# Order of work where the gate and value layer begins: square-sum matmul one step later, a fifth split buffer, S4 and first pair sums deferred, narrowing at five steps

## The chip, the core and the metric

One core of one Trainium2 chip. The metric is the device time of one execution in microseconds; the median of three runs of the kernel before is 578.98 us. Engines are called TensorE (PE in the rows; PEld is its weight load), VectorE (DVE), ScalarE (ACT), GpSimd (POOL) and SyncE (SP), whose queue issues nearly all DMAs.

## What is computed

Causal attention (2 batches, 12 heads, 448 positions, head size 64), then two feed-forward layers over the 896 tokens. Weights arrive as float64 and the output is float32. The two layers, cut from the reference:

```
h = x @ w_in;  x = (h * np.clip(h + 3.0, 0.0, 6.0) / 6.0) @ w_out      # 768 -> 2048 -> 768
rms = np.sqrt(np.mean(x * x, axis=-1, keepdims=True) + 1e-06)
xn = x / rms * rms_g
g = xn @ w_gate;  val = xn @ w_val                                     # 768 -> 1536, twice
out = (g * (1.0 / (1.0 + np.exp(-g))) * val) @ w_out2                  # 1536 -> 768
```

## The kernel before

Features lie on the partitions and tokens on the free axis, in two halves g = 0 and 1 of 448 tokens. Every float32 product is made of three matmuls of 128x128 by 128x448 (`mm3`): weight high part by data high part (L204 of the program before), high by low (L206), low by high (L208). So each weight and each operand has to be split beforehand: a ScalarE cast gives the high part (`whi`, `yhi`), a VectorE subtraction the low part (`wlo`, `ylo`).

A weight piece of 128x768 goes through: a load of 768 KB (`raw`, three buffers, shared with the pieces `braw` of w_out2 and `praw` of the later gate and value weights), the narrowing from float64 by two ScalarE passes (L155, L159) and a VectorE join (L164), then the split (L180, L186). `w_low` issues the load three pieces ahead. Pieces used a second time, for token half 1, come back as float32 (`c`) from a copy in memory (`kept`). `whi` and `wlo` have NW = 4 buffers each.

The order is written out by hand. All engines' work is emitted in steps; a step holds nine matmuls behind the attention, and `at(d, f)` puts f into the step d steps on. What a step emits for an engine stands ahead of that step's matmuls, and each engine works off its own list in order. The stages on TensorE are attention beside the first layer for half 0 (`ff1_in`), `ff1_in` for half 1, `ff1_out` for halves 0 and 1 (tiles y0_0 to y0_5 and y1_0 to y1_5, 16 x 3 matmuls each, weights 32 to 47 and 48 to 63), the gate/value layer's plain part `ff2_plain` (tiles f, 18 matmuls each, weights 64 to 69), its part by Strassen's scheme (`ff2_strassen`, three matmuls times three for each product), and the last layer (`strassen`).

`ff2_plain` goes through f0_0 to f0_3, f1_0 to f1_3, then f0_4, f1_4, f0_5, f1_5 (first number the token half, second the weight less 64; even is gate, odd value). A gate tile goes through Silu on ScalarE (`ff2_gate`), a value tile is multiplied to it on VectorE (`ff2_val`).

The norm of a token half: ScalarE scales and squares each y tile (`ff1_y`), the squares are added up, one matmul n with a matrix of ones sums over the partitions (`rms_sum`, L596), a square root on ScalarE and a reciprocal on VectorE follow (`rms_root`, L600, L601), then products with y (`y_scale`, L613) and splits (`y_split`, `y_low`, L626). For half 0 this lies far ahead of its use; for half 1 n is issued inside f0_0 and the first tile that reads its result is f1_0. Operands of the Strassen part are differences and sums of y tiles (`y_sums`, `y_more`): sets 5, 7, 6 and 3, the last (S4) read last. `sums_first` and `sums_second` make such sums of the finished gate-value products, in pairs p, and store them for the last layer (`left`).

`b_prepare` loads a piece of w_out2, `b_narrow` narrows it, `b_join` and `b_sums` derive seven matrices from it and store them (`kept`). Twelve pieces are taken, six beside `ff1_in` of half 1 and six beside `ff1_out` of half 1 (every 3.7 steps).

Of the kernel before, what the change touches and what calls it, by code (L numbers as in the profile page):

```python
# [21 lines left out]
NK = DM // 128  # L22
# [10 lines left out]
PLAIN = 3  # L33
MASK = -8e9
NRAW, NC_BUF, NW = 3, 3, 4
# [14 lines left out]
def fused_kernel(ctx: ExitStack, tc, qa, qb, ka, kb, v, w_in, w_out, w_gate, w_val, w_out2, rms_g, out):  # L50
# [38 lines left out]

    def begin_step():  # L90
        now = clock["now"]
        while due[now]:
            fn, args = due[now].pop(0)
            fn(*args)
        del due[now]
# [18 lines left out]
    apart = {n: APART for n in range(NW - 1)}  # L114
# [97 lines left out]
    def b_prepare(column, part):  # L212

        raw = wpool.tile([128, 768, 2], U32, tag="raw", name=f"braw{column}_{part}", bufs=NRAW)
        nc.sync.dma_start(raw.rearrange("p n t -> p (n t)"), w_out2[2 * column + part].bitcast(U32))
        at(3, b_narrow, column, part, raw)
# [224 lines left out]
    def ff1_out(g, w0):  # L441


        for m in range(NK):
            ps = psum(f"y{g}_{m}")[:, :NT]
            for k in range(NF1):
                i = m * NF1 + k
                yield from mm3(ps, w_tile(w0 + i // 6, i % 6), gs[g, k], k == 0, k == NF1 - 1)
            at(1, ff1_y, g, m, ps)
        for k in range(NF1):  # L450
            gs.pop((g, k))
# [11 lines left out]
    def left_ready(g, m, t):  # L463
# [6 lines left out]
        if all((i, 2 * p + j) in left for i in range(2) for j in range(2)):  # L470
            at(1, sums_first, p)
# [105 lines left out]
    def ff1_y(g, m, ps):  # L577
# [5 lines left out]
        if m == 0:  # L583
            ri[g] = s
        elif m < NK - 1:
            at(1, rms_add, g, s)
        else:
            nc.vector.tensor_add(ri[g], ri[g], s)
            at(1, rms_sum, g)
# [9 lines left out]
    def rms_root(g, ps):  # L599
        nc.scalar.activation(ri[g], ps, AF.Sqrt, bias=eps, scale=1.0 / DM)  # L600
        nc.vector.reciprocal(ri[g], ri[g])  # L601
        for i, k in enumerate((0, 1, 2, 3, 4, 5)):
            at(1 + (i // 2 if g else 2 * i), y_scale, g, k)
# [35 lines left out]
    def y_more(j):  # L639
        a11, a12 = ys.pop((0, j)), ys.pop((0, j + KH))  # L640
        nc.vector.tensor_sub(a11, ys.pop((1, j + KH)), a11)
        nc.vector.tensor_sub(a12, a12, a11)
        at(1, y_split, 6, j, a11)
        at(2, y_split, 3, j, a12)
# [4 lines left out]
    def ff2_plain(w0):  # L649
# [3 lines left out]
        for t, (g, i) in enumerate(order):  # L653
# [3 lines left out]
            if t == 0:  # L657
                at(1, w_split)
            elif t in (5, 6) or t >= 8 and t % 2 == 0:
                splits.pop(w0 + (t - 5 if t < 8 else i - 1), None)  # L660
                at(1, w_split)
            elif t == 7:
                splits.pop(w0 + 2)
# [115 lines left out]
    def ff2_strassen():  # L779
# [7 lines left out]
        for q, m in order:  # L787
            if q == 1 and m + 1 < NF2:
                pair_begin(m + 1)
            if q == 1 and m + 1 == NF2:  # L790
# [3 lines left out]
                for n in range(NW - 1):  # L794
                    at(4 + n, w_split)
# [74 lines left out]
    def products():  # L870
# [3 lines left out]
        yield from ff1_out(0, 2 * NP1)  # L874
        plan_preps(PREPS[0][2], *PREPS[1])
# [5 lines left out]
    with tc.manual_schedule():  # L881
# [40 lines left out]
        for n in range(NW - 1):  # L922
# [74 lines left out]
```

## Time and profile before

| | us |
|---|---|
| median of three runs | 578.98 (578.37 to 579.11) |
| the profiled execution's own time | 582.0 |
| its span, first to last instruction | 580.2 |
| TensorE busy | 566.5 (98%) |
| VectorE busy | 409.5 (71%) |
| ScalarE busy | 376.0 (65%) |
| GpSimd busy | 105.1 (18%) |
| mean granted TensorE clock | 0.994 of full |
| DMA | 125.59 MB, mean 216 GB/s |

The rows come from the one profiled execution, so sums of rows stand against 582.0 and not against the median. Times in a row count from the start of the span. A matmul's duration in a row includes its pipeline; the distance from one start to the next is what TensorE spends on it.

### The profile page before, as it was taken

The numbers are of one execution on the slowest core, as the hardware profiler recorded it, in microseconds if no ns is written. First come the engines' busy times: TensorE is split into PE (matmuls) and PEld (weight loads), VectorE is DVE, ScalarE is ACT, GpSimd is POOL, SyncE is SP. The second block draws the span as 40 slices with busy tenths as digits, with TensorE's granted clock in tenths as the row PEclk, the third lists the DMA queues.
The fourth block names the chain that finished last, engine by engine and source line by source line (L and its number), as shares of the span: only waits on it lengthen the run. The fifth ranks groups of instructions, "written<-read, shape, count | busy, mean of one in ns | idle before, by whom it ended". The sixth has DMA issues, their size and how long they took to land.

```text
span 580.2 us, 9124 instructions
## 1 busy us (share of the span) xinstructions
PE 566.5 (98%) x3057; PEld 493.6 (85%) x3057; DVE 409.5 (71%) x783; ACT 376.0 (65%) x740; POOL 105.1 (18%) x148
## 2 busy tenths in 40 slices
PE   8899999999999999999999989899999999999997
PEld 6457777777899999999999779799999999999996
DVE  4766777776467786555585679988797887865871
ACT  7997888887576588776564776546555555554540
POOL 4665535353000000010010100120112110000000
PEclk9999999999999999999999999899999999999999
DMA  8958776753369889985687842373654647576751
GB/s 235 280 186 248 223 250 199 250 177 111 132 218 298 292 295 323 326 317 203 215 297 246 323 156 87 113 253 121 201 175 162 206 153 260 171 237 205 266 183 63
DMA packets 51231, 125.59 MB, mean 216 GB/s; under 512 B 6768, under 2 KB 30256, under 8 KB 51184
## 3 DMA queue, kind: packets, MB, share of 16 engines
q1 hardware_dynamic: 50752, 124.66, 64.3%
q8 instruction: 24, 0.39, 0.3%
q10 hardware_dynamic: 432, 0.34, 0.2%
q14 instruction: 23, 0.19, 0.1%
HBM read 93.36 MB, written 31.62 MB: 215 GB/s over the span
## 4 chain that ended last, share of the span: by engine, by line
PE 82%; DVE 6%; DMA 4%; ACT 4%; SPq 3%; issue 2%; DVEq 0%
PE h L208 7%; PE h L204 7%; PE h L206 7%; PE y L208 6%; PE y L204 6%; PE y L206 6%; PE f L208 4%; PE f L204 4%; PE f L206 4%; PE o L391 3%; PE t L365 3%; PE s L314 3%; PE fr L208 2%; PE fx L204 2%; PE fx L208 2%; PE fr L206 2%
## 5 line engine op out<-in xcount | busy, mean ns | idle before, releaser
L186 DVE TENSOR_TENSOR wlo<-c,whi 128x768 fp32r<-128x768 f32 x91 | 90.4, 996 | 24.2 <-ACT whi L180 21.7
L180 ACT CAST whi<-c 128x768 fp32r<-128x768 f32 x91 | 76.1, 837 | 46.9 <-DVE c L164 25.9
L208 PE MATMUL h<-xh,wlo 128*128 128x448 f32 x192 | 72.0, 375 | 0.0
L204 PE MATMUL y<-ghi,whi 128*128 128x448 f32 x192 | 70.5, 367 | 0.6 <-ACT whi L180 0.6
L208 PE MATMUL y<-ghi,wlo 128*128 128x448 f32 x192 | 70.5, 367 | 0.5 <-DVE wlo L186 0.5
L206 PE MATMUL h<-xl,whi 128*128 128x448 f32 x192 | 70.9, 369 | 0.0
L204 PE MATMUL h<-xh,whi 128*128 128x448 f32 x192 | 70.4, 367 | 0.0
L206 PE MATMUL y<-glo,whi 128*128 128x448 f32 x192 | 69.4, 361 | 0.0
L349 POOL TENSOR_SCALAR sm<-sm,st 112x112 f32<-112x112 f32 (+1 forms) x96 | 55.9, 600 | 68.3 <-ACT pt L375 28.8
L331 ACT ACTIVATE sm<-sm,st 112x112 f32<-112x112 f32 (+3 forms) x96 | 49.9, 532 | 3.5 <-DVE st L324 3.4
L164 DVE SCALAR_TENSOR_TENSOR c<-c,raw 128x768 uint32<-128x768 uint32 x38 | 38.5, 1014 | 18.6 <-ACT raw L159 12.4
L208 PEld LDWEIGHTS h<-xh,wlo 128*128 128x128 f32 x192 | 36.0, 188 | 9.3 <-issue 6.7
L592 POOL TENSOR_TENSOR sq<-sq,sq 128x448 f32<-128x448 f32 x8 | 10.3, 1286 | 175.4 <-DVE c L164 94.7
L157 POOL TENSOR_SCALAR praw<-praw 128x768 uint32<-128x768 uint8 x18 | 19.3, 1074 | 122.7 <-DMA praw<-in_w_gate 74.9
L324 DVE CUSTOM_DVE_ANT_0 sm<-s,mask 112x112 f32<-112x112 f32 (+3 forms) x96 | 37.3, 443 | 5.9 <-PE s L314 5.7
L208 PEld LDWEIGHTS y<-ghi,wlo 128*128 128x128 f32 x192 | 35.9, 187 | 5.0 <-DVE wlo L186 1.6
L204 PEld LDWEIGHTS y<-ghi,whi 128*128 128x128 f32 x192 | 36.0, 188 | 3.5 <-ACT whi L180 1.0
L206 PEld LDWEIGHTS h<-xl,whi 128*128 128x128 f32 x192 | 36.0, 188 | 2.8
L206 PEld LDWEIGHTS y<-glo,whi 128*128 128x128 f32 x192 | 36.0, 188 | 2.8
L204 PEld LDWEIGHTS h<-xh,whi 128*128 128x128 f32 x192 | 36.2, 188 | 2.5
L428 DVE SCALAR_TENSOR_TENSOR t<-t,h 128x448 f32<-128x448 f32 x32 | 19.8, 618 | 24.5 <-ACT t L424 24.5
L365 PE MATMUL t<-ident,sm 112*112 112x112 f32 x240 | 33.1, 269 | 2.9 <-POOL sm L349 2.4
(169 smaller groups left out, 1353.7 us busy)
## 6 DMA issues: line engine op xcount, KB each, us to landing
raw<-in_w_in SPq DMA_DIRECT2D x16, 768.0 KB, 5.3
raw<-in_w_out SPq DMA_DIRECT2D x16, 768.0 KB, 6.3
braw<-in_w_out SPq DMA_DIRECT2D x12, 768.0 KB, 7.0
c<-kept SPq DMA_DIRECT2D x21, 384.0 KB, 3.3
a<-left SPq DMA_DIRECT2D x35, 224.0 KB, 3.9
praw<-in_w_gate SPq DMA_DIRECT2D x9, 768.0 KB, 4.4
praw<-in_w_val SPq DMA_DIRECT2D x9, 768.0 KB, 5.7
keptin<-c SPq DMA_DIRECT2D x16, 384.0 KB, 2.7
```

The lines of the kernel that those rows point to most:

```text
L157: nc.gpsimd.tensor_scalar(low, byte, 1.0 / 32.0, -15.5 / 32.0, op0=ALU.mult, op1=ALU.add)
L164: nc.vector.scalar_tensor_tensor(bits, bits, 3, z, ALU.logical_shift_left, ALU.bitwise_or)
L180: nc.scalar.copy(hi, c)
L186: nc.vector.tensor_sub(lo, c, f32(hi))
L204: nc.tensor.matmul(ps, whi, xhi, start=first, stop=False, skip_group_check=again)
L206: nc.tensor.matmul(ps, whi, xlo, start=False, stop=False, skip_group_check=again)
L208: nc.tensor.matmul(ps, wlo, xhi, start=False, stop=last, skip_group_check=again)
L324: nc.vector.tensor_tensor_reduce(dst, src, mask[:, S - n:], scale=-0.125, scalar=3e38, op0=ALU.add, op1=ALU.min, accum_out=st[u][:, 0, c:c ...
L331: nc.scalar.activation(dst, dst, AF.Exp, scale=-1.0, bias=st[u][:, 0, c:c + 1], accum_out=st[u][:, 1, c:c + 1])
L349: nc.gpsimd.tensor_scalar(t[:, o:o + n], t[:, o:o + n], c, 1.0, op0=ALU.mult, op1=ALU.mult)
L365: nc.tensor.transpose(banks[-1][:C, o:o + C], t[:, o0 + kc * C:o0 + (kc + 1) * C], ident[:C, :C])
L428: nc.vector.scalar_tensor_tensor(t, t, 1.0, ps, ALU.min, ALU.mult)
```

## The change

It edits the order at several places, and one count of buffers:

- NW goes from 4 to 5, with one more `w_split` emitted as `ff1_out` of half 1 begins; every later split then runs one piece further ahead. `ff2_plain` and `ff2_strassen` have their calls of `w_split` rearranged for that. Where NW - 1 = 3 stood for the first splits, NRAW = 3 stands now, the same number.
- `b_narrow` comes five steps after the load instead of three, for all twelve pieces.
- `ff1_y` is put at the head of the next step (`soon`) instead of behind what is there.
- `rms_sum` comes a step later.
- S4 (the last subtraction of `y_more`, now `y_last`) and its split come 12 and more steps later.
- The sums of the first pair (`sums_first(0)`) come 12 steps later instead of one.

What it does to the lists of the engines, at three places. The first is ScalarE's list beside `ff1_out` of half 1 (y1), before and after. The names braw4_1 and braw5_1 are the last two pieces of w_out2, whi59 to whi63 the casts of weights for y1.

```order
L180 CAST whi59_3660<-c59_3565 128x768
L180 CAST whi60_3696<-c60_3598 128x768
L155 ACTIVATE braw5_1_3672<-braw5_1_3672 128x768
L159 ACTIVATE braw5_1_3672<-braw5_1_3672 128x768
L180 CAST whi61_3723<-c61_3634 128x768
L579 ACTIVATE y1_3_3726<-y1_3_3618,gvec_74 128x448
L581 ACTIVATE sq1_3_3728<-y1_3_3618 128x448
L180 CAST whi62_3761<-c62_3683 128x768
L180 CAST whi63_3793<-c63_3709 128x768
```

```order
L184 CAST whi60_3650<-c60_3560 128x768
L159 ACTIVATE braw4_1_3590<-braw4_1_3590 128x768
L163 ACTIVATE braw4_1_3590<-braw4_1_3590 128x768
L184 CAST whi61_3692<-c61_3599 128x768
L583 ACTIVATE y1_3_3725<-y1_3_3617,gvec_74 128x448
L585 ACTIVATE sq1_3_3727<-y1_3_3617 128x448
L184 CAST whi62_3731<-c62_3634 128x768
L159 ACTIVATE braw5_1_3662<-braw5_1_3662 128x768
L163 ACTIVATE braw5_1_3662<-braw5_1_3662 128x768
L184 CAST whi63_3758<-c63_3671 128x768
```

The casts whi61 and whi62, and y1_3's passes, stood behind the narrowing of braw5_1 and now stand ahead of it; the same holds for the earlier pieces.

The second is where half 1's norm begins. TensorE's list, with n1 the square-sum matmul and f0_0, f0_1 the first gate and value tile, before and after:

```order
L206 MATMUL f0_0_3884<-ylo2_2_3595,whi64_3836 128x448
L596 MATMUL n1_3916<-sq1_0_3424,ones_70 128x448
L208 MATMUL f0_0_3884<-yhi2_2_3594,wlo64_3837 128x448
L204 MATMUL f0_1_3920<-yhi1_0_3399,whi65_3864 128x448
L206 MATMUL f0_1_3920<-ylo1_0_3400,whi65_3864 128x448
```

```order
L210 MATMUL f0_1_3922<-ylo1_2_3491,whi65_3846 128x448
L600 MATMUL n1_3931<-sq1_0_3414,ones_70 128x448
L212 MATMUL f0_1_3922<-yhi1_2_3490,wlo65_3847 128x448
L208 MATMUL f0_1_3922<-yhi2_0_3532,whi65_3846 128x448
L210 MATMUL f0_1_3922<-ylo2_0_3533,whi65_3846 128x448
```

n1 moved by nine matmuls, from f0_0 into f0_1. ScalarE's list behind it, from the square root before, and from the Silu of f0_0 (t0_0) after:

```order
L600 ACTIVATE sq1_0_3424<-n1_3916,eps_73 128x448
L180 CAST whi67_3931<-c67_3901 128x768
L685 ACT_TABLE_LOAD
L685 ACTIVATE t0_0_3934<-f0_0_3884 128x448
L619 CAST yhi0_0_3960<-y1_0_3422 128x448
L619 CAST yhi0_1_3963<-y1_1_3523 128x448
L619 CAST yhi0_2_3980<-y1_2_3636 128x448
L619 CAST yhi4_0_3983<-y1_3_3726 128x448
L619 CAST yhi4_1_3998<-y1_4_3812 128x448
```

```order
L695 ACTIVATE t0_0_3933<-f0_0_3894 128x448
L604 ACT_TABLE_LOAD
L604 ACTIVATE sq1_0_3414<-n1_3931,eps_73 128x448
L623 CAST yhi0_0_3972<-y1_0_3412 128x448
L623 CAST yhi0_1_3975<-y1_1_3506 128x448
L623 CAST yhi0_2_3990<-y1_2_3626 128x448
L623 CAST yhi4_0_3993<-y1_3_3725 128x448
L695 ACT_TABLE_LOAD
L695 ACTIVATE t0_1_3998<-f0_2_3947 128x448
L159 ACTIVATE c68_4000<-raw68_3862 128x768
L163 ACTIVATE raw68_3862<-raw68_3862 128x768
L623 CAST yhi4_1_4012<-y1_4_3805 128x448
```

The Silu of f0_0 moved ahead of the square root, which adds two table loads, and the narrowing of weight 68 (c68, raw68) moved ahead of the last two casts (yhi4_1, yhi4_2) that f1_0 reads.

The third is VectorE's list around wlo68, the low part of the weight that f0_4 reads, before and after; ylo5, ylo6, ylo7 and ylo3 are operands of the Strassen part, ylo4 of f1_0.

```order
L690 TENSOR_TENSOR t1_0_4078<-f1_1_4054,t1_0_4078 128x448
L626 TENSOR_TENSOR ylo3_1_4121<-y0_4_3253,yhi3_1_4120 128x448
L626 TENSOR_TENSOR ylo6_2_4127<-y0_2_3091,yhi6_2_4126 128x448
L186 TENSOR_TENSOR wlo68_4131<-c68_4080,whi68_4130 128x768
L164 SCALAR_TENSOR_TENSOR c69_4133<-c69_4133,raw69_3914 128x768
L626 TENSOR_TENSOR ylo3_2_4148<-y0_5_3334,yhi3_2_4147 128x448
L186 TENSOR_TENSOR wlo69_4169<-c69_4133,whi69_4168 128x768
```

```order
L630 TENSOR_TENSOR ylo4_0_3994<-y1_3_3725,yhi4_0_3993 128x448
L168 SCALAR_TENSOR_TENSOR c68_4000<-c68_4000,raw68_3862 128x768
L630 TENSOR_TENSOR ylo4_1_4013<-y1_4_3805,yhi4_1_4012 128x448
L630 TENSOR_TENSOR ylo4_2_4016<-y1_5_3903,yhi4_2_4015 128x448
L637 TENSOR_TENSOR y1_3_3725<-y1_0_3412,y1_3_3725 128x448
L638 TENSOR_TENSOR y1_0_3412<-y0_0_2912,y1_0_3412 128x448
L700 TENSOR_TENSOR t0_1_3998<-f0_3_3979,t0_1_3998 128x448
L190 TENSOR_TENSOR wlo68_4034<-c68_4000,whi68_4033 128x768
```

wlo68 moved from behind the split passes of the Strassen operands to the place right behind the product t0_1 of f0_3; the passes ylo3 went far behind it.

The diff:

```diff
--- before.py
+++ after.py
@@ -31,8 +31,9 @@
 NSLOT = 79
 PREPS = (2, 4, 6), (1, 3.7, 6)
 PLAIN = 3
+LATE = 12
 MASK = -8e9
-NRAW, NC_BUF, NW = 3, 3, 4
+NRAW, NC_BUF, NW = 3, 3, 5
 
 BESIDE, AFTER = 4.8, 9
 APART = 4
@@ -86,6 +87,9 @@
 
     def at(delay, fn, *args):
         due[clock["now"] + delay].append((fn, args))
+
+    def soon(fn, *args):
+        due[clock["now"] + 1].insert(0, (fn, args))
 
     def begin_step():
         now = clock["now"]
@@ -111,7 +115,7 @@
     srcs += [(p, n) for p in ORDER for n in range(NN)]
     raws, plain, splits = {}, {}, {}
 
-    apart = {n: APART for n in range(NW - 1)}
+    apart = {n: APART for n in range(NRAW)}
     state = {"load": 0, "split": 0, "limit": OUT2}
 
     def w_load():
@@ -213,7 +217,7 @@
 
         raw = wpool.tile([128, 768, 2], U32, tag="raw", name=f"braw{column}_{part}", bufs=NRAW)
         nc.sync.dma_start(raw.rearrange("p n t -> p (n t)"), w_out2[2 * column + part].bitcast(U32))
-        at(3, b_narrow, column, part, raw)
+        at(5, b_narrow, column, part, raw)
 
     def b_narrow(column, part, raw):
         c = f32(raw[:, :, 1])
@@ -446,7 +450,7 @@
             for k in range(NF1):
                 i = m * NF1 + k
                 yield from mm3(ps, w_tile(w0 + i // 6, i % 6), gs[g, k], k == 0, k == NF1 - 1)
-            at(1, ff1_y, g, m, ps)
+            soon(ff1_y, g, m, ps)
         for k in range(NF1):
             gs.pop((g, k))
 
@@ -468,7 +472,7 @@
         if q:
             left_keep(q, p, t)
         if all((i, 2 * p + j) in left for i in range(2) for j in range(2)):
-            at(1, sums_first, p)
+            at(1 if p else LATE, sums_first, p)
 
     def sums_first(p):
 
@@ -586,7 +590,7 @@
             at(1, rms_add, g, s)
         else:
             nc.vector.tensor_add(ri[g], ri[g], s)
-            at(1, rms_sum, g)
+            at(2, rms_sum, g)
 
     def rms_add(g, s):
         nc.gpsimd.tensor_add(ri[g], ri[g], s)
@@ -599,8 +603,8 @@
     def rms_root(g, ps):
         nc.scalar.activation(ri[g], ps, AF.Sqrt, bias=eps, scale=1.0 / DM)
         nc.vector.reciprocal(ri[g], ri[g])
-        for i, k in enumerate((0, 1, 2, 3, 4, 5)):
-            at(1 + (i // 2 if g else 2 * i), y_scale, g, k)
+        for k in range(NK):
+            at(1 + (k // 2 if g else 2 * k), y_scale, g, k)
         if g:
             for j in range(KH):
                 at(6 + j, y_sums, j)
@@ -637,11 +641,15 @@
         at(1, y_more, j)
 
     def y_more(j):
-        a11, a12 = ys.pop((0, j)), ys.pop((0, j + KH))
+        a11 = ys.pop((0, j))
         nc.vector.tensor_sub(a11, ys.pop((1, j + KH)), a11)
-        nc.vector.tensor_sub(a12, a12, a11)
         at(1, y_split, 6, j, a11)
-        at(2, y_split, 3, j, a12)
+        at(LATE + j, y_last, j, a11)
+
+    def y_last(j, s2):
+        a12 = ys.pop((0, j + KH))
+        nc.vector.tensor_sub(a12, a12, s2)
+        at(1, y_split, 3, j, a12)
 
 
     ss, spare = {}, []
@@ -654,13 +662,15 @@
             m, n = divmod(i, 2)
             if t < 2:
                 splits.pop(w0 + t - 2, None)
-            if t == 0:
+            if t == 3:
                 at(1, w_split)
-            elif t in (5, 6) or t >= 8 and t % 2 == 0:
-                splits.pop(w0 + (t - 5 if t < 8 else i - 1), None)
+            elif t == 5:
+                splits.pop(w0)
                 at(1, w_split)
-            elif t == 7:
-                splits.pop(w0 + 2)
+            elif t in (6, 7):
+                splits.pop(w0 + t - 5)
+            elif t in (8, 10):
+                splits.pop(w0 + i - 1)
             if t == len(order) - 6:
                 at(1, pair_load, PLAIN, 0)
                 at(2, pair_load, PLAIN, 1)
@@ -792,7 +802,7 @@
                 for n in range(NRAW):
                     at(1 + n, w_load)
                 for n in range(NW - 1):
-                    at(4 + n, w_split)
+                    at(4 + n + 3 * (n // 3), w_split)
                 for p in range(NF2 // 2):
                     at(1 + p // 2, a_fetch, ORDER[0], p)
                     at(4 + p // 2, a_split, ORDER[0], p)
@@ -872,6 +882,7 @@
         plan_preps(0, *PREPS[0])
         yield from ff1_in(1, NP1)
         yield from ff1_out(0, 2 * NP1)
+        at(1, w_split)
         plan_preps(PREPS[0][2], *PREPS[1])
         yield from ff1_out(1, 3 * NP1)
         yield from ff2_plain(IN2)
@@ -919,7 +930,7 @@
         for n in range(NRAW):
             plan[12 + 12 * n].append((1, w_load))
             plan[52 + 6 * n].append((1, w_load))
-        for n in range(NW - 1):
+        for n in range(NRAW):
             plan[26 + 12 * n].append((0, w_split))
 
         work = products()
```

## Rows read from the trace of the kernel before

**Rows 1.** The page, part 1: busy us, share of the span, instructions.

```profile
PE 566.5 (98%) x3057; PEld 493.6 (85%) x3057; DVE 409.5 (71%) x783; ACT 376.0 (65%) x740; POOL 105.1 (18%) x148
```

**Rows 2.** TensorE's waits: who waited for whom, us, times, longest.

```profile
PE f L208 <- DVE wlo L186: 2.0, 1, 2.0
PE n L596 <- DVE sq L588: 1.9, 1, 1.9
```

**Rows 3.** Timeline of TensorE, 337 to 353: start, us, operation, [idle before <-releaser].

```profile
338.07 0.36 PE L206 MATMUL f<-ylo,whi 128*128 128x448 f32 x1
340.29 1.02 PE L596 MATMUL n<-sq,ones 128*128 128x448 f32 x2 [1.86 <-DVE sq L588]
...
341.35 0.36 PE L204 MATMUL f<-yhi,whi 128*128 128x448 f32 x1
...
352.27 0.36 PE L204 MATMUL f<-yhi,whi 128*128 128x448 f32 x1
```

**Rows 4.** Timeline of TensorE, 310 to 325.

```profile
311.06 0.36 PE L206 MATMUL y<-glo,whi 128*128 128x448 f32 x1
...
311.74 0.36 PE L204 MATMUL y<-ghi,whi 128*128 128x448 f32 x1
...
321.84 0.37 PE L208 MATMUL y<-ghi,wlo 128*128 128x448 f32 x1
322.81 0.47 PE L204 MATMUL y<-ghi,whi 128*128 128x448 f32 x1 [0.60 <-ACT whi L180]
...
324.02 0.47 PE L208 MATMUL y<-ghi,wlo 128*128 128x448 f32 x1 [0.54 <-DVE wlo L186]
324.33 0.37 PE L204 MATMUL y<-ghi,whi 128*128 128x448 f32 x1
```

**Rows 5.** Timeline of TensorE, 366 to 378.

```profile
367.03 0.37 PE L206 MATMUL f<-ylo,whi 128*128 128x448 f32 x1
369.40 0.65 PE L208 MATMUL f<-yhi,wlo 128*128 128x448 f32 x1 [2.00 <-DVE wlo L186]
...
373.09 0.36 PE L204 MATMUL f<-yhi,whi 128*128 128x448 f32 x1
```

**Rows 6.** Stretch 370:371: busy (x) by engine, PEclk, DMA share, GB/s.

```profile
370.00:371.00 1.00, 1.00 (x5) 0.87 (x4) 0.75 (x2) 0.70 (x1) 1.00 (x1) 0.50 0.00 0
```

**Rows 7.** Timeline of ScalarE, 304 to 330.

```profile
320.35 0.91 ACT L155 ACTIVATE braw<-braw 128x768 f32<-128x768 f32 x1 [8.06 <-DMA braw<-in_w_out]
321.16 0.88 ACT L159 ACTIVATE braw<-braw 128x768 uint32<-128x768 uint8 x1
```

**Rows 8.** DMA issues: xcount, KB each, median us to landing.

```profile
braw<-in_w_out SPq DMA_DIRECT2D x12, 768.0 KB, 7.0
...
raw<-in_w_gate SPq DMA_DIRECT2D x3, 768.0 KB, 6.4
```

**Rows 9.** Timeline of VectorE, 335 to 395.

```profile
342.02 2.95 DVE L601 RECIPROCAL sq<-sq 128x448 f32<-128x448 f32 x1
...
346.08 0.95 DVE L186 TENSOR_TENSOR wlo<-c,whi 128x768 fp32r<-128x768 f32 x1
...
349.62 3.30 DVE L626 TENSOR_TENSOR ylo<-y,yhi 128x448 fp32r<-128x448 f32 x6
...
368.39 0.95 DVE L186 TENSOR_TENSOR wlo<-c,whi 128x768 fp32r<-128x768 f32 x1
```

**Rows 10.** Timeline of ScalarE, 335 to 395.

```profile
341.35 0.64 ACT L600 ACTIVATE sq<-n,eps 128x448 f32<-128x448 f32 x1 [0.24 <-PE n L596]
...
342.99 1.28 ACT L685 ACT_TABLE_LOAD   x1
344.28 0.55 ACT L685 ACTIVATE t<-f 128x448 f32<-128x448 f32 x1
...
347.60 2.18 ACT L619 CAST yhi<-y 128x448 fp32r<-128x448 f32 x4 [0.83 <-DVE y L613]
```

**Rows 11.** Timeline of SP's DMA queue, 310 to 340.

```profile
334.11 0.33 SPq L124 DMA_DIRECT2D raw<-in_w_gate  x1
```

## The prediction, made blind

> **What bounds the kernel now.** I read the page first: TensorE is busy for 98% of the span [rows 1], so the only time that can be won is time in which it stands or is granted less clock. Second, its list of waits: the two longest single ones are a wait of 2.0 us for wlo and one of 1.9 us for the square-sum, each happening once [rows 2]. Third, the timeline of TensorE around these places, which gives the loss in steps between matmuls. A matmul normally starts 0.202 us after the one before: from 341.35 to 352.27 there are 54 of them [rows 3]. Four places lose time, all between 311 and 373 us.
>
> - y half 1, output tile 4, wlo58: 311.06 to 311.74 is two steps, 0.68 instead of 0.40 us: 0.28 lost [rows 4].
> - The same tile, whi61 and then wlo61: 321.84 to 324.33 is four steps, 2.49 instead of 0.81: 1.68 lost [rows 4].
> - The square-sum matmul n of half 1: after the matmul at 338.07 it should start at 338.27 and starts at 340.29: 2.02 lost [rows 3].
> - The gate tile f of half 0, fifth column, wlo68: 367.03 to 373.09 is eleven steps, 6.06 instead of 2.22: 3.84 lost [rows 5]. Only some 2.2 us of this is the wait. After TensorE had stood there, the granted clock was 0.50, the 1.2 GHz level of the two (2.4 is the other) [rows 6]; the steps stay slow until 373.09. A wait that goes takes this tail with it.
>
> Together 7.82 us. What ended each wait is on other engines. At 320.35 ScalarE had stood 8.06 us for the load of a w_out2 piece [rows 7]: the narrowing is placed three steps after the load's issue, a step is nine matmuls, so 5.5 us, and such a load takes 7.0 us at the median [rows 8]. The cast of whi61 stood behind it. The square-sum waited because ScalarE squares the last y tile only at the end of a chain of narrowings that the same late start pushed back. wlo68 was last in a VectorE queue that runs without a gap from the reciprocal at 342.02 to 368.39 [rows 9].
>
> **The change part by part.**
>
> *Narrowing at five steps, and one split more in flight.* Five steps are 9.1 us, over the 7.0 us of the load [rows 8]. In the order, whi59 to whi62 each move ahead of a narrowing that they followed, and the fifth buffer and the additional split at the start of the y half 1 move each split two steps (3.6 us) forward. So whi61 no longer waits for the load of the last piece, and I book 0.28 + 1.68 = 1.96 us. What this adds is that a raw buffer is held two steps longer, and SP's loads of the next raw pieces stand behind that release. The pieces come 3.7 steps apart through three buffers, so one is due again after 11 steps and is released after 6. The stores of the derived pieces move later on SP's queue by the same two steps; nothing reads them until the last layer. I cost both at 0, with the two steps (3.6 us) as cover. In the first half, where the same delay is applied, TensorE has no wait now and none is booked; the bounds are 0 and what is lost at a like place, 1.68 us.
>
> *Square-sum a step later.* n moves nine matmuls back, 1.82 us, and y and its square are now put at the head of their step. ScalarE's two passes for y (not moved on TensorE) come before the last cast of w. The margin becomes 1.82 us from the move and some 3.6 us from the earlier chain, against a wait of 2.02. It goes: 2.02 us. n and everything that hangs on it stay; the question is what is late next, since the products of half 1 now start earlier after n: 352.27 less 340.29 is 11.98 us now [rows 3], and 11.98 - 1.82 = 10.16 us after the change.
>
> Count from n's start. The square root starts at +1.06 [rows 3, 10]. The order puts a Silu and a table load in front of it, which are new there. The Silu needs the gate tile that ends 1.62 us before n (eight matmuls); Silu 0.55 and load 1.28 [rows 10] end at about +0.4. So it is hidden by 0.6 us. The reciprocal takes +1.73 to +4.68 (342.02, 2.95 long) [rows 9]. The first ylo started at 349.62, +9.33 [rows 9]; the pass of wlo67 that lay before it (0.95 long, 0.87 of the queue) [rows 9] is now done earlier, so +8.46, finished by +9.1. TensorE reads it with its second matmul, +10.36. The last two ylo are the tight ones, since the order puts the second new table load, a Silu, both narrowing passes of the next weight and their join in front of them. On ScalarE the fourth yhi ends at about +7.5 (four products 0.54 apart after +4.7, then its own 0.57); load 1.28, to +8.8; Silu 0.55, to +9.35; two passes of 0.91 and 0.88 [rows 7], overlapping by a tenth, to +11.0; VectorE's join, 0.95 as for a tile of this size [rows 9], to +12.0; the fifth ylo to +12.6. Its reader is the 14th matmul of the tile, 10.16 + 13 x 0.202 = +12.8. So it is hidden by 0.2 us, and the sixth by about as much. I take 0. The other end is a lateness of about 1 us if ScalarE is half a microsecond later at two places.
>
> The Trainium skill, "ScalarE: Activation LUTs", section "What ACT_TABLE_LOAD costs", gives 1.28 us for the load and a further 1.38 us of drain for each switch of table set. The trace agrees on the load alone: it ends at 344.27 and the Silu starts at 344.28, with nothing between [rows 10]. By the Trainium skill's figure the change would end near the time of the second rival.
>
> *S4, pair sums and their stores later.* Three subtractions and two split passes leave VectorE's queue ahead of wlo68, and the split of weight 68 is issued two tiles (7.3 us) earlier: wlo68 now stands right behind the product of the fourth tile. In the count above that is near +15, and its reader comes four tiles after the first of half 1, at 10.16 + 14.6 = +24.8. So 3.84 us go, tail included. The deferred passes, ten of about 0.6 us on VectorE (the four sums among them) and three casts on ScalarE, land in the stretch from 375 to 395, where the order has them before their readers by 6 us or more; I cost them at 0. The four stores leave SP's queue ahead of the loads of the next pairs, which can only come sooner.
>
> *The sum.* 1.96 + 2.02 + 3.84 = 7.82 us gained, nothing booked against it. The profiled execution took 582.0 us, so 574.2 on its scale. The median of the runs is 578.98, 3.0 us less than that, so some of the waits may be shorter without the profiler. I choose the whole sum, because the two largest terms hang on the order of queues and not on a load: 578.98 - 7.82 = 571.2.
>
> **The rivals.**
>
> *The waits on loads are smaller in a plain run.* The missing 3.0 us would lie in the terms that hang on loads (1.96 and 2.02). Then only 7.82 - 3.0 = 4.8 us are to be had: 574.2. For it speaks the 8.06 us stand of ScalarE, which rests on a single slow load [rows 7]. Against it: the 3.0 us can lie anywhere in the first 50 us too.
>
> *A new wait before the first tile of half 1.* The cover is 0.2 us. Suppose each switch of table held ScalarE for twice its row, 1.28 us more. The first load would end at -0.5 instead of -1.8, the Silu at 0.0, the second load at +2.6, so the square root 1.5 us late, and the last casts another 1.3: 2.8 us. TensorE would wait 2.6 us there and then run at the lower clock as after 369.40, another 1.67 (3.84 less 2.17): 571.2 + 4.3 = 575.5. Against it: the Silu that follows the load at once [rows 10]. The drain in the Trainium skill's page "ScalarE: Activation LUTs" would be such a hold.
>
> *The wait moves.* If the next weight (69) or the pair after it inherited the lateness of wlo68 and the square root that of n, the kernel would stay at about 579.0. Against it: the queue ahead of these got shorter too.
>
> *Slower, by the load of weight 68.* Its narrowing now stands on ScalarE ahead of two casts that the first tile of half 1 reads, where it stood far behind them. If that load landed late, TensorE would stand behind it one for one. It is issued at 334.11 [rows 11], takes 6.4 us at the median [rows 8], so lands by 340.5, and is needed at about 347.5. It decides from there on: to end slower than 578.98 by 1.2 us, the wait must be 7.82 + 1.2 - 1.67 = 7.35 us, so a landing at about 355. No load in the trace is near that.
>
> **How the numbers follow.** Forecast 0.70 (571.2, itself 570.0 to 572.5); smaller waits 0.15 (574.2); new wait 0.06 (575.5); the wait moves 0.05 (579.0); slower 0.04 (580.2 or more). The first two hold 0.85, so the range goes from 569.9 to 575.2. A measurement of this kernel tells 0.2%, 1.2 us, from no change: faster 0.70 + 0.15 + 0.06 = 0.91, the same 0.05, slower 0.04.
>
> **What would show it.** Right: in the list of waits of TensorE none for wlo, whi or the square-sum is left, the granted clock stays at 1.00 through 360 to 380, ScalarE's rows have two more table loads of 1.28 us, and the first tile of half 1 starts some 10.2 us after n. Wrong: a step over 0.3 us at the fifth or sixth ylo of half 1, ScalarE still standing before a braw pass with a whi cast late behind it, or a half-clock stretch anywhere behind 60 us.

## The result, and the profile after

The changed kernel takes **574.74 us** (median, 574.29 to 576.65, 7 runs). The kernel before, timed beside it, takes 580.19 us (578.37 to 582.13, 7 runs). The ratio is 0.991, with an interval from 0.9886 to 0.9933: 0.9% faster. The prediction's 571.2 us is 3.5 us too low; its range, 569.9 to 575.2, holds the time, and "faster by over 0.2%" was right. The profiled execution took 575.0 us, span 572.9, against 582.0 and 580.2 before: 7.3 us of span.

The page of after, part 1, answers [rows 1] (busy us, share of the span, instructions):

```profile
PE 564.0 (98%) x3057; PEld 493.3 (86%) x3057; DVE 410.1 (72%) x783; ACT 377.2 (66%) x742; POOL 104.9 (18%) x148
```

Two instructions more on ScalarE, the two table loads; otherwise the same work. TensorE's list of waits is given whole, against [rows 2]:

```profile
PE t L369 <- POOL sm L353: 2.0, 2, 1.4
PE warm L899 <- DVE ones L893: 1.1, 1, 1.1
PE o L395 <- ACT pt L379: 1.0, 1, 1.0
PE o L395 <- DMA v<-in_v: 0.8, 1, 0.8
PE s L318 <- ACT pt L379: 0.2, 1, 0.2
```

All five lie in the first 45 us, the attention. None for wlo, whi or n is left. The windows of the stretch where [rows 6] had shown a granted clock of 0.50 (PEclk is the third value from the end):

```profile
360.00:370.00 10.00, 10.00 (x52) 9.27 (x51) 9.97 (x16) 4.82 (x8) 1.47 (x2) 1.00 0.19 58
370.00:380.00 10.00, 10.00 (x51) 9.28 (x50) 9.62 (x15) 5.30 (x10) 2.42 (x2) 1.00 0.55 207
```

The clock stays at 1.00. ScalarE behind the square-sum, the timeline that answers [rows 10] (start, us, operation, [idle before]):

```profile
336.16 1.28 ACT L695 ACT_TABLE_LOAD   x1
337.45 0.54 ACT L695 ACTIVATE t<-f 128x448 f32<-128x448 f32 x1
338.01 1.28 ACT L604 ACT_TABLE_LOAD   x1
339.63 0.64 ACT L604 ACTIVATE sq<-n,eps 128x448 f32<-128x448 f32 x1 [0.33 <-PE n L600]
343.94 2.17 ACT L623 CAST yhi<-y 128x448 fp32r<-128x448 f32 x4 [3.68 <-DVE y L617]
346.13 1.28 ACT L695 ACT_TABLE_LOAD   x1
347.43 0.55 ACT L695 ACTIVATE t<-f 128x448 f32<-128x448 f32 x1
347.87 0.91 ACT L159 ACTIVATE c<-raw 128x768 f32<-128x768 f32 x1
348.68 0.89 ACT L163 ACTIVATE raw<-raw 128x768 uint32<-128x768 uint8 x1
349.46 1.02 ACT L623 CAST yhi<-y 128x448 fp32r<-128x448 f32 x2
```

The two Silu start 0.01 and 0.02 us after the end of their loads; the square root waits 0.33 us for n, not for the load ahead of it. So the added loads cost TensorE nothing in this execution; where ScalarE is late they do (only_sum, below).

Where the time went is seen by stages. The table gives distances between the starts of TensorE's first matmul in two tiles, from the timeline, in us; "y1" is y1_0 to f0_0, "n" f0_0 to f0_2, "f1" f0_2 to f0_4, "wlo68" f0_4 to f1_4, "rest" f1_4 to fx_8 (the first product of pair 8), "total" y1_0 to the last matmul's end; what follows fx_8 takes 129.4 us in every kernel. A number in bold is above the lowest of its column by over 0.05. The experiments of the next section stand below the first two rows.

| kernel | y1 | n | f1 | wlo68 | rest | total |
|---|---|---|---|---|---|---|
| before | **61.13** | **10.16** | 21.84 | **7.47** | **73.07** | **303.07** |
| after | 58.99 | 8.04 | 21.84 | 3.64 | **73.12** | **295.04** |
| only_narrow | 58.99 | 8.04 | 21.84 | **5.90** | 72.84 | **297.02** |
| early_load | 58.99 | 8.04 | 21.84 | **7.47** | 72.84 | **298.59** |
| only_defer | **60.79** | **11.77** | 21.84 | 3.64 | 72.83 | **300.28** |
| only_buffer | 58.99 | **17.88** | 21.84 | 3.64 | 72.84 | **304.60** |
| only_sum | **62.87** | 8.03 | **24.69** | **8.60** | 72.83 | **306.43** |
| narrow_defer | 58.99 | 8.04 | 21.84 | 3.64 | 72.84 | 294.75 |
| changed_again | 58.99 | 8.04 | 21.84 | 3.64 | **73.37** | **295.28** |
| undo_narrow | 58.99 | **10.54** | **23.98** | 3.64 | 72.83 | **299.39** |
| undo_buffer | 58.99 | 8.04 | **23.79** | **4.52** | 72.84 | **297.59** |
| undo_defer | 58.99 | 8.04 | 21.84 | 3.64 | **74.41** | **296.33** |
| undo_sum | 58.99 | 8.04 | 21.84 | 3.64 | **72.93** | **294.85** |
| undo_sum_again | 58.99 | **9.55** | 21.84 | 3.64 | **73.20** | **296.63** |

From before to after, 2.14 + 2.12 + 3.83 us went out of the three stages that the prediction had named, against 1.96, 2.02 and 3.84 booked. In the trace the total fell by 8.03 us; 0.72 us of it was lost again ahead of these stages (the first-layer tile h0_1 starts at 52.30 before, at 53.02 after), where the change moves nothing; from 20 to 30 and from 30 to 40 us the granted clock was 0.80 and 0.86 after, 0.91 and 0.92 before.

### The profile page after: what moved, and what is told of

Read it like the earlier page. It is cut to its first block, busy times and chain, and to the rows that moved or that the text cites. A ratio compares the mean times of both kernels' runs of the same rounds, so it can differ in the third digit from the quotient of the medians.

```text
span 572.9 us, 9099 instructions
## 1 busy us (share of the span) xinstructions
PE 564.0 (98%) x3057; PEld 493.3 (86%) x3057; DVE 410.1 (72%) x783; ACT 377.2 (66%) x742; POOL 104.9 (18%) x148
## 4 chain that ended last, share of the span: by engine, by line
PE 94%; DMA 3%; SPq 2%; ACT 1%; issue 0%; DVE 0%
PE y L208 8%; PE y L212 8%; PE y L210 8%; PE h L212 7%; PE h L208 7%; PE h L210 7%; PE f L208 5%; PE f L212 5%; PE f L210 5%; PE t L369 4%; PE o L395 4%; PE s L318 4%; PE fr L212 2%; PE fx L208 2%; PE fx L212 2%; PE fr L210 2%
## 5 line engine op out<-in xcount | busy, mean ns | idle before, releaser
L428 ACT ACTIVATE t<-h,half 128x448 f32<-128x448 f32 x32 | 20.4, 638 | 25.5 <-PE h L212 25.5
```

## The experiments

Two questions were open. Which of the four parts carries the gain? And do the waits hang on a load, or on the order of queues? The prediction gave the square-sum a term of its own and held that the two largest terms did not hang on a load. Four kernels take one part back out of the whole change, four put one part alone into the kernel before, and the last four test what these showed. Kernels of one group were timed on one chip, each group on another, beside the same runs of before: the undo group at 580.9 us (17 runs), the only group at 580.75 (19), the last at 580.64 (29). Ratios are to before, with their intervals.

**Taking one part back.** Narrowing at three steps again:

```diff
-        at(5, b_narrow, column, part, raw)
+        at(3, b_narrow, column, part, raw)
```

> The changed kernel with the narrowing of w_out2 pieces back at three steps. ScalarE stands again before the pieces, but whi61 is now ahead of the last one. Theory Q: no wait of TensorE for whi61 or wlo61; the chain of 64 to 67 starts later and n may wait: 0 to 1 us over the changed kernel. Rival N (the five steps are what pays at y half 1): +1.7 us or more, with a wait for whi or wlo in the list.

580.86 us (579.22 to 583.61), ratio 0.9995 (0.9977 to 1.0013): without it nothing of the gain is left. TensorE's waits behind the attention, in the list of waits:

```profile
PE n L600 <- DVE sq L592: 2.2, 1, 2.2
PE f L210 <- DVE ylo L630: 1.5, 2, 0.8
```

n waits 2.2 us although it stands a step later, so the step alone does not remove that wait. The y stage lost nothing: the earlier splits already cover whi61 (table, 58.99), as the first expectation had it; but the cost is well over the 0 to 1 us that it gave.

The square-sum and the y passes back at their old places:

```diff
-            soon(ff1_y, g, m, ps)
+            at(1, ff1_y, g, m, ps)
...
-            at(2, rms_sum, g)
+            at(1, rms_sum, g)
```

> The changed kernel with the square-sum matmul and the y passes back at their old steps; the two added table loads go with that. Theory Q: n stands 17 matmuls into f0_0 and its sum is ready about 1 us later than that, so a wait of about 1 us for the square-sum, +1.0 us over the changed kernel. Rival S (the step is worth the whole old wait): +2.0. Rival T (the added table loads cost time that the trace hides): 0 or faster than the changed kernel.

574.25 us (573.43 to 575.1), ratio 0.9879 (0.9853 to 0.9905), no wait behind the attention. The part that was booked at 2.02 us is not missed.

The fifth buffer and the places of the splits (the core of the edit):

```diff
-NRAW, NC_BUF, NW = 3, 3, 5
+NRAW, NC_BUF, NW = 3, 3, 4
...
-        at(1, w_split)
         plan_preps(PREPS[0][2], *PREPS[1])
```

> The changed kernel with four split buffers and the old places of the splits. Counting VectorE's passes from the reciprocal as the rows give them, wlo68 ends 24.8 us after n's start and is read at 25.1. Theory Q: the deferral alone just frees wlo68, and the later narrowing frees whi61, so 0 to 0.8 us over the changed kernel. Rival B (the fifth buffer is what pays): wlo68's wait and tail are back, +3.8 us, or whi61's, +1.7.

577.31 us (577.04 to 578.05), ratio 0.9931 (0.9908 to 0.9955). New waits:

```profile
PE f L212 <- DVE wlo L190: 1.5, 2, 0.9
PE f L210 <- DVE ylo L630: 0.6, 1, 0.6
```

The wlo are those of weight 67 and 68 (0.85 and 0.61 us by the timeline). The cost, 2.6 us, fits neither expectation. The kernel narrow_defer, below, has neither the buffer nor the later square-sum, and none of these waits: the buffer is needed only beside a square-sum that comes 1.8 us later.

S4 and the first pair sums not deferred:

```diff
-            at(1 if p else LATE, sums_first, p)
+            at(1, sums_first, p)
...
-        at(LATE + j, y_last, j, a11)
+        nc.vector.tensor_sub(a12, a12, a11)
+        at(2, y_split, 3, j, a12)
```

> The changed kernel with S4 and the first pair sums back at their old steps. Theory Q (each wait is a matter of the queue's order, and weight 68's split already stands early through the fifth buffer): wlo68 stays some 10 us ahead of its reader, wlo69 comes about 2 us later than in the changed kernel but still ahead of f0_5, so 0.0 to 0.3 us over the changed kernel, granted clock 1.00 at 360 to 380. Rival D (the deferral is what frees wlo68): the wait of 2.0 us and the half-clock tail come back, +3.8 us.

575.92 us (575.64 to 576.21), ratio 0.9907 (0.9884 to 0.993). One wait is added, at 382.61 us, and it isn't for wlo68:

```profile
PE f L208 <- ACT f L824: 1.3, 1, 1.3
```

This is the copy of a finished tile from one bank to another, with which a Strassen group begins (`ff2_combine`, q = 1). With the split issued early, wlo68 is in time whether or not S4 stands ahead; in this trace the deferral then pays in another place (rest, 74.41 against 72.84). In the ratios, 0.9907 here and 0.991 for the whole change, nothing of it can be told.

**One part alone.** Narrowing at five steps in the kernel before:

```diff
-        at(3, b_narrow, column, part, raw)
+        at(5, b_narrow, column, part, raw)
```

> The kernel before with the narrowing at five steps and nothing else. Theory L (ScalarE's stands for loads are what pays and what makes the times scatter): no wait for whi61 or wlo61, the wait for the square-sum under 1 us, wlo68's wait of about 2 us and the half-clock tail stay; 3 to 4 us under the kernel before, and its runs lie within 1.5 us of each other, where those of the kernel before lie 4.9 us apart. Rival Q (order of queues, loads do not matter): 2 us under the kernel before, the same scatter.

577.47 us (576.35 to 577.83), ratio 0.9941 (0.9921 to 0.9962). One wait is left behind the attention:

```profile
PE f L208 <- DVE wlo L186: 2.0, 1, 2.0
```

So this part alone, 3.3 us, takes the waits in y1 and the one at n, with n at its old place.

Deferral alone:

```diff
-            at(1, sums_first, p)
+            at(1 if p else LATE, sums_first, p)
...
-        nc.vector.tensor_sub(a12, a12, a11)
...
-        at(2, y_split, 3, j, a12)
+        at(LATE + j, y_last, j, a11)
```

> The kernel before with S4 and the first pair sums deferred alone. Counting passes, wlo68 ends 3.1 us earlier in VectorE's queue, 1 us ahead of its reader. The prediction's step (the deferral frees wlo68): no wait for wlo68, no half-clock tail, 3.8 us under the kernel before. Rival E (earlier split frees it, the deferral pays elsewhere, at the copy that the first Strassen group waits for): wlo68's wait stays above 1 us, 0 to 1.5 us under the kernel before. In both the scatter of the kernel before.

577.83 us (575.65 to 580.14), ratio 0.9952 (0.9928 to 0.9977). The wait for wlo68 is gone, the others stand:

```profile
PE n L597 <- DVE sq L589: 1.9, 1, 1.9
PE y L209 <- DVE wlo L187: 0.7, 2, 0.5
```

The buffer and the splits alone (the core of the edit):

```diff
-NRAW, NC_BUF, NW = 3, 3, 4
+NRAW, NC_BUF, NW = 3, 3, 5
...
+        at(1, w_split)
         plan_preps(PREPS[0][2], *PREPS[1])
```

> The kernel before with the fifth buffer, the additional split and the rearranged splits alone. Theory L: ScalarE still stands for the loads, so the chain of 64 to 67 is late, the square-sum waits 2 us or more and the times scatter by over 3 us; wlo68 has no wait any more: 2 to 4 us under the kernel before. Rival B (the buffer alone frees the y1 stretch, wlo68 and the chain): 6 us under it.

583.37 us (580.98 to 586.28), ratio 1.0045 (1.0025 to 1.0064): slower, where both expectations had it faster. The waits in y1 and for wlo68 are gone (table, 58.99 and 3.64), but n waits longer, and behind the wait the granted clock is 0.50:

```profile
PE n L596 <- DVE sq L588: 6.9, 1, 6.9
```

Its ScalarE timeline shows why: the last y tile's passes, before n, start at 341.06, behind four narrowings of gate and value weights (two passes each, from 326.27, 330.60, 334.06 and 337.58); in the kernel before they start at 338.44, behind three. Earlier splits push the squares back as long as the narrowings of w_out2 ahead of them are late.

The later square-sum alone, with the y passes at the head:

```diff
-            at(1, ff1_y, g, m, ps)
+            soon(ff1_y, g, m, ps)
...
-            at(1, rms_sum, g)
+            at(2, rms_sum, g)
```

> The kernel before with the later square-sum matmul and the y passes at the head of their step alone. The prediction's step: n's wait of 2 us goes, wlo68's wait stays at 2 us with its tail, 2.0 us under the kernel before. Rival L: the sum is not late by itself but through ScalarE's stand, the products of half 1 then come earlier after n and wait instead: 0 to 1 us under the kernel before. The scatter of the kernel before in both.

587.23 us (586.39 to 588.43), ratio 1.0115 (1.0093 to 1.0137): slower by 6.5 us.

```profile
PE f L211 <- DVE wlo L189: 4.9, 2, 3.1
PE y L211 <- DVE wlo L189: 2.8, 3, 1.2
PE f L209 <- DVE ylo L629: 0.6, 1, 0.6
```

Neither expectation had this. n no longer waits, but what follows it is later against readers that did not move, and wlo67 and wlo68 are late. The square root of half 1 starts 4.2 us after n (347.01 and 342.78 us), against 1.06 before: a cast, and then the two table loads with the Silu between them (343.86 to 347.01), stand ahead of it, and wlo67 stands behind the reciprocal that follows. Here the added loads are not hidden. The step moves half 0's square-sum too: its square root comes behind the first narrowing beside y1, for whose load ScalarE had stood 5.93 us, and starts at 285.57 against 278.10 before; TensorE then waits 0.99 us, at 291.52, for a wlo behind that reciprocal. The other two waits in y1 were not followed. The four single parts give -3.3, -2.9, +2.6 and +6.5 us: they do not add up to -5.5.

**Load or order?** The narrowing at five steps does two things: the load has time to land, and casts of weights stand ahead of narrowings on ScalarE. This kernel is the one before, with the second six pieces loaded two steps earlier and narrowed where they were; ScalarE's list beside y1 is that of before. (The first six, beside `ff1_in` of half 1, where TensorE has no wait, are loaded where they were and narrowed two steps later.)

```diff
-PREPS = (2, 4, 6), (1, 3.7, 6)
+PREPS = (2, 4, 6), (31, 3.7, 6)
...
-        at(3, b_narrow, column, part, raw)
+        at(5, b_narrow, column, part, raw)
...
-        yield from ff1_out(0, 2 * NP1)
         plan_preps(PREPS[0][2], *PREPS[1])
+        yield from ff1_out(0, 2 * NP1)
```

> The kernel before, with the six w_out2 pieces taken beside ff1_out of half 1 loaded two steps (3.6 us) earlier and narrowed at the old places: five steps lie between load and narrowing there, but ScalarE's list in ff1_out of half 1 is word for word that of before (whi59 to whi62 behind the narrowings). It tells apart why narrowing at five steps alone gained 3.3 us. Theory A, ScalarE no longer stands for a load: the same gain comes without moving anything on ScalarE, 577.4 against 580.7 for before, a scatter of about 1.5 us as with only_narrow, and no wait of TensorE for whi61 or n, only wlo68's 2 us. Theory B, the casts had to stand ahead of the narrowing: time and scatter of before, within 1 us of it, with waits in y1 or at n.

577.41 us (576.32 to 583.5), ratio 0.9953 (0.9932 to 0.9974): the median of only_narrow. Nothing is lost in y1 or at n (table), and one wait is left behind the attention, that for wlo68. ScalarE's first narrowing pass in the stretch 270 to 323, grouped by line (count | busy, mean ns | idle before, releaser), for before, early_load, after and only_buffer:

```profile
L155 ACT ACTIVATE braw<-braw 128x768 f32<-128x768 f32 x6 | 5.5, 917 | 19.8 <-DMA braw<-in_w_out 19.8
```

```profile
L155 ACT ACTIVATE braw<-braw 128x768 f32<-128x768 f32 x6 | 5.5, 913 | 2.1 <-DMA braw<-in_w_out 2.1
```

```profile
L159 ACT ACTIVATE braw<-braw 128x768 f32<-128x768 f32 x6 | 5.5, 914 | 2.2 <-DMA braw<-in_w_out 2.2
```

```profile
L155 ACT ACTIVATE braw<-braw 128x768 f32<-128x768 f32 x6 | 5.5, 909 | 18.4 <-DMA braw<-in_w_out 18.3
```

ScalarE stood 19.8 us for these six loads before, 2.2 after. The loads did not become quicker: from issue to landing the six took 4.9 to 7.6 us before and 4.6 to 9.4 after. For this edit the theory that the load's time is what pays is borne out, and the one on the place of the casts falls. The place of the casts is a second remedy, for y1 alone: in only_buffer ScalarE stands 18.4 us as before, each cast comes one split sooner, and y1 loses nothing (58.99), while n waits 6.9 us.

Why the loads were so late is seen on SP's queue, before (start, us, issue):

```profile
308.09 0.32 SPq L261 DMA_DIRECT2D kept<-b  x1
311.40 0.32 SPq L133 DMA_DIRECT2D c<-keptout  x1
311.77 0.90 SPq L261 DMA_DIRECT2D kept<-bt  x2
312.71 0.47 SPq L215 DMA_DIRECT2D braw<-in_w_out  x1
```

and in SP's list of waits of the same kernel from 304 to 318:

```profile
SPq L261 <- DVE b L230: 4.1, 1, 4.1
SPq L133 <- DVE wlo L186: 2.9, 1, 2.9
```

The load at 312.71, for which ScalarE then stood 8.06 us until 320.35 [rows 7], was itself issued behind a store of the piece two before it and behind a load of c that waited for a wlo. The store was late because ScalarE had stood 5.66 us, until 305.29, for that earlier piece; the load at 312.71 then took 7.6 us, no more than others. One late load delays a later one. In early_load the last such load goes out at 305.79, 26.1 us after y1_0 where before it went out 39.0 us after, and the store that stood ahead of it (kept<-b) at 306.77, behind it. The Trainium skill, "DMA: Bandwidth & Descriptors", section "Anatomy of one DMA — SWDGE (gpsimd) path", says that a wait on a semaphore happens on the issuing sequencer before the transfer is handed over. The rows above, on SP's queue, agree: 4.1 and 2.9 us of waits stand ahead of this load.

**Two parts in place of four.** Narrowing at five steps and the deferral, put into the kernel before:

```diff
-        at(3, b_narrow, column, part, raw)
+        at(5, b_narrow, column, part, raw)
...
-            at(1, sums_first, p)
+            at(1 if p else LATE, sums_first, p)
...
-        at(2, y_split, 3, j, a12)
+        at(LATE + j, y_last, j, a11)
```

> The kernel before with two parts of the change alone: narrowing at five steps, and S4 with the first pair sums deferred; four split buffers, the old places of the splits and of the square-sum. Theory A, the late start of the narrowings and the queue ahead of wlo68 are all that was lost: no wait of TensorE is left behind 150 us, 574.3, like the whole change (the queue count puts the end of wlo68 some 25.9 us after the square-sum and its read at 26.9). Theory B, the fifth buffer is needed, as taking it out of the whole change cost 2.6 us: 576.9, with a wait for wlo68.

574.24 us (573.56 to 574.61), ratio 0.9896 (0.9864 to 0.9929). wlo68 is done 1.34 us ahead of its reader (done 361.92, read 363.26). No wait of TensorE is left behind the attention, and its total in the table, 294.75, is what the lowest number of every column and the 129.4 us behind them add up to (294.7): against the best of these traces nothing is lost in any stage.

**The whole change, and it without the later square-sum, side by side.** The first is the changed kernel as it is:

> The whole change once more, on the same chip as the next kernel: 574.7 by its first timing. Beside the kernel before in the same call it shows how large the gain is, 5.5 us by the first timing and 7.8 by the sum of the prediction.

575.04 us (574.18 to 579.98, 12 runs), ratio 0.9909 (0.9883 to 0.9934): the first result again. The second has the edit of undo_sum once more:

> The whole change with the square-sum and y passes at their old places, on the same chip as the whole change. Theory A, the later square-sum is not needed once the narrowings start in time: the same within 0.2% (1.1 us). Theory B, the second pair of table loads, which only the later square-sum brings, costs something that the first timing saw (574.25 against 574.74): 0.5 us faster, with intervals that separate. Prediction's step, the later square-sum gains 2.0 us: slower by 2.0.

575.22 us (573.62 to 580.89, 12 runs), ratio 0.9915 (0.9885 to 0.9946): no difference of medians that can be told, so neither the 2.0 us of the prediction's step nor the 0.5 of the first timing. In this profiled execution n did wait:

```profile
PE n L600 <- DVE sq L592: 1.2, 1, 1.2
```

ScalarE had stood 2.80 us for a load of a gate weight ahead of the squares there. In the first profiled execution of the same edit n did not wait. So the later square-sum is a margin against a late load: of the two profiled executions without it one lost 1.2 us of waiting there, the other nothing. With the highest run of each left out, 11 runs span 574.18 to 575.57 with it and 573.62 to 576.98 without.

narrow_defer is the quickest of the last group, 0.8 us below the whole change on the same chip (undo_sum, on another, has the ratio 0.9879 against 0.9896, with intervals that overlap). That is less than the 0.2% (1.2 us) which the prediction took as the limit of a measurement, but all but one of the 12 runs of the whole change lie above the highest of its 6. Part of it is seen in the trace of the whole change, in its second profile: TensorE waits for a copy of the kind that undo_defer had shown, and ScalarE makes that copy behind a narrowing for whose load it had stood 4.91 us.

```profile
PE f L208 <- ACT f L828: 0.3, 1, 0.3
```

```profile
405.56 0.91 ACT L159 ACTIVATE pc<-praw 128x768 f32<-128x768 f32 x1 [4.91 <-DMA praw<-in_w_val]
406.38 0.56 ACT L854 ACTIVATE c<-c 128x448 f32<-128x448 f32 x1
406.85 0.52 ACT L828 COPY f<-fx 128x448 f32<-128x448 f32 x1
```

The rest of the 0.8 us stays open.

## Why the prediction was right, and where not

- **What bounds the kernel**: right. All that went, went at the places that the prediction had found by the steps between matmuls: 2.14 + 2.12 + 3.83 = 8.09 us in the trace against 7.82.
- **Narrowing at five steps and one split more, booked at 1.96**: right in y1, and too small. The text had joined two remedies, and each alone frees y1: the narrowing (only_narrow, early_load) and the earlier split (only_buffer, undo_narrow). The narrowing alone gave 3.3 us, twice over (only_narrow, early_load), since n's wait goes with it. The prediction had itself written that the square-sum waits at the end of a chain that the same late start pushed back; it should have put that term here. It also took ScalarE's stand for that of a load of 7.0 us against a distance of 5.5, which makes 1.5 us, and the 8.06 us for a single slow load. The load took 7.6 us; it was issued late, and six loads made ScalarE stand 19.8 us.
- **Square-sum a step later, booked at 2.02**: wrong. Without the step the time is the same (undo_sum, undo_sum_again); with it and late narrowings n still waits 2.2 us (undo_narrow). Alone it costs 6.5 us. The margin of 1.82 + 3.6 us was counted from a trace in which the loads, not the place of n, made it late.
- **S4 and sums, booked at 3.84, tail included**: right in its place and its tail, with two causes where the text had joined them. The deferral alone removes the wait (only_defer, narrow_defer), and so does the earlier split alone (only_buffer, undo_defer). On top of the narrowing the deferral gives 6.40 us against before less 3.28, 3.1 us. The tail was counted as if it always came with the wait: in only_narrow the same wait lost 2.26 us and not 3.83. Booking the ten deferred passes at 0 held: narrow_defer has them and loses nothing behind f1_4 (72.84).
- **No new wait at f1_0**: right. f1_0 starts at 348.73, 10.05 us after n at 338.68, against 10.16 forecast. The last two ylo are done 0.27 and 0.35 us ahead of their readers, against 0.2. The square root was hidden, as foreseen. The drain of 1.38 us that the Trainium skill, "ScalarE: Activation LUTs", section "What ACT_TABLE_LOAD costs", adds to each load is not seen behind any of the three loads: the next instruction starts 0.01 and 0.02 us after two of them, and after the third it waits 0.33 us for n.
- **"The two largest terms hang on the order of queues and not on a load"**: this sentence failed, and with it the choice of the whole sum. n's wait hung on a load (in early_load ScalarE's list beside y1 is that of before, and the wait is gone), and it differed between two executions of one edit: none in undo_sum, 1.2 us in undo_sum_again. The rival "waits on loads are smaller in a plain run", 574.2, has the number that came out, with a chance of 0.15; that it came so near is in part luck, since its reason can explain only a part of what was missing, as the next paragraph counts.

The missing 3.5 us of the first result, taken on the last group, where all were timed together: 575.04 less 571.16 is 3.88. Of these, 1.66 is the base: 580.64 in 29 runs, where the three runs that the prediction subtracted from gave 578.98 (the other four of the first result lie from 580.19 to 582.13). Then 7.82 less 6.40 (580.64 less 574.24, narrow_defer, which has none of the booked waits), 1.42: the profiled execution of before seems to have lost more than a typical one, since its 582.0 us lies 1.36 above that median. What it lost more is not shown; the tail behind wlo68, 1.57 us in this execution and absent in only_narrow, is one candidate of that size. The last 0.80 is the distance of the whole change from narrow_defer. Subtracting the sum from 582.0, its own execution, would have given 574.2; the prediction named both and chose the lower.

## What to carry to other kernels

Where an engine stands for a load, ask first when the load was issued and what stood ahead of it in the issuing queue; here one narrowing's lateness delayed a later load, and two steps of distance between load and use broke that loop. Waits that share a cause belong in one term: undoing one edit of the bundle showed in one run that the step booked at 2.0 us was worth nothing there. And a sum of waits from one execution goes with that execution's own time, not with the median of three other runs.

## What the runs showed of the hardware beyond this

**A wait of 2.0 us costs 2.3 or 3.8.** wlo68 made TensorE stand 2.00 us in before, only_narrow and early_load. In early_load, as in before [rows 6], the granted clock then fell to 0.50, the lower of its two levels (1.2 GHz); in only_narrow it stayed at 1.00. One-us windows right behind the wait (PEclk third from the end), only_narrow and early_load:

```profile
366.00:367.00 1.00, 1.00 (x6) 0.93 (x7) 1.00 (x2) 0.25 (x1) 1.00 (x1) 1.00 0.00 0
367.00:368.00 1.00, 1.00 (x7) 0.93 (x6) 0.58 (x2) 1.00 (x3) 0.96 (x1) 1.00 0.00 0
```

```profile
371.00:372.00 1.00, 0.87 (x4) 0.80 (x5) 1.00 (x3) 0.00 (x0) 0.95 (x1) 0.87 0.00 0
372.00:373.00 1.00, 1.00 (x4) 0.92 (x3) 0.58 (x2) 0.97 (x2) 1.00 (x1) 0.50 0.00 0
```

The stage took 5.90 and 7.47 us against 3.64 undisturbed. The wait for n did the same: 1.86 us in before lost 2.12, with 1.00 behind it; 1.85 us in only_defer lost 3.73, with 0.50 from 342 to 344 us. What decides between the two was not tried.

**The start of the kernel scatters by more than the change.** h0_1 started at 52.58 in narrow_defer and at 58.33 in early_load, with the attention's work the same. Windows of 30 to 40 us, narrow_defer and early_load:

```profile
30.00:40.00 10.00, 9.24 (x65) 5.24 (x61) 6.49 (x32) 10.00 (x38) 8.15 (x17) 1.00 0.49 152
```

```profile
30.00:40.00 10.00, 10.00 (x56) 6.11 (x53) 5.88 (x29) 8.19 (x32) 6.83 (x13) 0.50 0.13 38
```

In early_load TensorE was granted half the clock there, though it was busy throughout; in the 10 us before, it was busy for 8.17 us in both. That execution has a span of 581.7 us, took 583.5 where the twelve others of its kernel took 576.32 to 578.58, and lost nothing in y1 or at n. So a single profile's span says little of such a change, and the stages had to be compared from y1_0 on.
